# Output tiles in token halves of 64: one gate operation for each PSUM bank, and each half split when it is complete

## The chip, the cores and the metric

The kernel runs on one core of a Trainium2 chip. The time is the device time of one execution in microseconds, the median of several runs; lower is better. TensorE does the matrix products, VectorE (DVE) and ScalarE (ACT) the elementwise work on SBUF and PSUM, GpSimd (POOL) some elementwise work on SBUF, and SyncE (SP) issues almost all DMAs. Each engine takes its instructions in the order in which the program wrote them.

## The reference

Two branches over the same 2048 tokens of 576 channels are mixed by a sigmoid gate. The first is a long convolution (a state-space kernel built from its parameters and applied by a Fourier transform). The second, cut to what matters:

```
s1, s2 = scores of 32 heads against 64 + 64 keys;  top 2 of each, best 2 of the 4 sums
top_e  = expert number (of 4096) of the 2 chosen per head, g = softmax of their scores
act = gelu(einsum("nd,nhkd->nhk", x, u[top_e]))
b   = einsum("nhk,nhk,nhkd->nd", g, act, v[top_e])
out = gate * a + (1 - gate) * b
```

Nothing is gathered. The kernel multiplies every token with all 4096 experts, applies GELU to all of it, multiplies by a gate matrix that is zero except at the chosen experts, and multiplies the result with all rows of `v`.

## The kernel before

The order of all instructions is set by a planner in the program itself. Generators wait for estimated ready times (`ready`), for free buffers (`need`, `take`, `free`) and are resumed by `pump` as the planner's clock advances with each matmul; costs of VectorE, ScalarE, GpSimd and DMA are estimated by the small functions at the top. The resulting order is fixed when the program is built; on the chip only semaphores decide the times.

The work around the change:

- The activations `a` (token tile against experts) are computed as 128 x 512 matmuls, scaled out of PSUM into `go` and stored to a DRAM scratch tensor `g_d` with shape [16 token tiles, 128, 32, 128]: expert row in the partition, 32 expert blocks, 128 tokens.
- `gating` makes, for each token tile, the transposed lists of chosen experts and their weights by small matmuls against an identity; `turned` copies them to `idxT` (partition: head and choice in two token groups; 64 columns).
- `prep(t)` makes the weights of one output tile of 128 tokens. It loads the tile of `g_d` into two slots `gl`, applies GELU on ScalarE, and in four quarters builds one-hot operands (`onehot`: `A`, `Be`, `Bg` on VectorE), multiplies them on TensorE into two PSUM banks `S` of 512 columns (the gates of 16 columns for all 4096 experts), and multiplies the banks into `gl` on VectorE. At the end the product is split into a high and a low float16 part `wh` by `split` (ScalarE the high part, VectorE the remainder; for the first two tiles in some cases ScalarE and GpSimd), and `st[t]` says that the tile is ready.
- The main loop multiplies `wh` of one tile with `v` (`vhl`, 8 chunks, themselves split from the raw rows; the last comes through the slot `vs`) into two banks `o`: 32 blocks x 3 products x 2 halves of the channels = 192 matmuls for a tile. Between blocks it calls `pump`, so that selections `S` of later tiles and the `y` matmuls of the convolution come between the products.
- There are 9 slots ("slot") for `gl`, `wh` and the operands of the earlier stages; one tile needs two for `gl` and two for `wh`.

The tiles are taken in the order 0, 15, 1, 14 and so on. "First", "second", "third" tile below is by this order. All helper calls of VectorE, ScalarE and GpSimd carry line 134 in the profile, all matmuls line 214, all DMAs line 205.

Of the kernel before, what the change touches and what calls it, by code (L numbers as in the profile page):

```python
# [12 lines left out]
F32 = mybir.dt.float32  # L13
# [125 lines left out]
def body(ctx: ExitStack, tc: tile.TileContext, xT, au, par, logdt, dskip, gatew, wq, kT, uT, vv,  # L139
# [60 lines left out]
    def dma(o, i, q=None):  # L200
        t = max(clock[0], rdy.get(key(i), 0.0), queue[0])
        queue[0] = t + 0.45
        wire[0] = max(wire[0], t) + (2 if o.dtype in (F16, BF16) else 4) * o.shape[0] * size(o) / 3.4e5
        rdy[key(o)] = max(rdy.get(key(o), 0.0), wire[0] + 2.2)
        (q or DQ).dma_start(o, i)

    def mm(o, l, r, start, stop, cost=None):
        m = l.shape[0] > 64, 128 if size(l) > 64 else size(l)
        if m != tiling[0]:
            tiling[0] = m  # L210
            clock[0] += 0.13 if m == (True, 128) else 0.1
        clock[0] += (size(r) * (4 if r.dtype == F32 else 1) / 2400 + 0.003) if cost is None else cost
        rdy[key(o)] = clock[0] + 0.4
        T.matmul(o, l, r, start=start, stop=stop)  # L214

    def spawn(gen, after=0.0):
        heapq.heappush(heap, (clock[0] + after, nseq[0], gen))
        nseq[0] += 1
# [16 lines left out]
    def ready(*xs, late=0.0):  # L235
        while True:
            t = max(rdy.get(key(x), 0.0) for x in xs) + late - clock[0]
            if t <= 0:
                return
            yield t  # L240
# [740 lines left out]
    def gating(c):  # L981

        while taken[c] < 4 or not ff:
            yield 0.5
        vv_ = vals[:, :, 8 * c:8 * c + 8].rearrange("p t (h s) k -> p t h s k", s=2)
        ii = idx[:, :, 8 * c:8 * c + 8].rearrange("p t (h s) k -> p t h s k", s=2)
        tl = lambda nm, *z: ff.tile([128, NT, 4, *z], F32, tag="gg" + nm, name=f"gg{nm}{c}")
        a0, a1, b0, b1 = vv_[:, :, :, 0, 0], vv_[:, :, :, 0, 1], vv_[:, :, :, 1, 0], vv_[:, :, :, 1, 1]
        u, w, s, d = tl("u"), tl("w"), tl("s"), tl("d")
        i1, i2, ib = tl("i1", 2), tl("i2", 2), tl("ib", 2)  # L990
        G.tensor_add(u, a0, b1)
        G.tensor_add(w, a1, b0)
# [24 lines left out]
        V.tensor_scalar(ib, ib, MAGIC, MAGIC, op0=OP.add, op1=OP.subtract)  # L1017
        V.scalar_tensor_tensor(i1, i2, 64.0, i1, op0=OP.mult, op1=OP.add)
        fl = lambda x: x.rearrange("p t h k -> p t (h k)")
        V.scalar_tensor_tensor(place[0][:, :, 8 * c:8 * c + 8], fl(ib), -128.0, fl(i1), op0=OP.mult, op1=OP.add)  # L1020
        S.activation(place[1][:, :, 8 * c:8 * c + 8], fl(ib), AF.Copy)
        V.tensor_scalar(u, d, 1.0, None, op0=OP.add)
        V.reciprocal(u, u)
        V.tensor_scalar(u, u, 2.0 ** 14, None, op0=OP.mult)
        pr = prob[:, :, 8 * c:8 * c + 8].rearrange("p t (h k) -> p t h k", k=2)
        yield from ready(u)
        S.activation(pr[:, :, :, 0], u, AF.Copy)
        G.tensor_mul(pr[:, :, :, 1], u, d)
        if c < 7:
            spawn(gating(c + 1))  # L1030
            return
        gated.append(1)
        yield from ready(vals)
        for t in range(NT):
            yield from need("wb")
            p = bank("wb", f"tr{t}")
            for r, x, i in ((0, place[0][:, t], identb), (1, place[1][:, t], identb), (2, prob[:, t], ident)):
                for hh in range(2):
                    mm(p[64 * hh:64 * hh + 64, 64 * r:64 * r + 64], x, i[:, 64 * hh:64 * hh + 64], True, True,
                       0.12 if r == 2 else 0.04)  # L1040
            spawn(turned(t, p))
            del p

# [436 lines left out]
    st = {}  # L1480
# [14 lines left out]
    def prep(t):  # L1495
        while stored[t // 4] < 32:
            yield 1
        yield from need("slot", 2)
        gl = [slot([16, 128], F32, f"gl{t}_{h}") for h in range(2)]
        for h in range(2):  # L1500
            dma(gl[h], g_d[t][:, 16 * h:16 * h + 16])
        while t not in placed:
            yield 0.3
        oh = {0: onehot(t, 0), 1: onehot(t, 1)}
        yield from ready(*gl)
        for h in range(2):
            for b0 in (0, 8):
                g = gl[h][:, b0:b0 + 8]
                S.activation(g, g, AF.Gelu_apprx_tanh)
        for q in range(4):  # L1510
            A, Bg = oh.pop(q)
            yield from ready(A, Bg)
            yield from need("wb", 2)
            pbs = []
            for hb in range(2):
                pS = bank("wb", f"S{t}_{q}_{hb}")
                for j in range(8):
                    a, k = 4 * hb + j // 2, j % 2
                    for z in range(2):
                        mm(pS[:, 64 * j:64 * j + 64], A[:, a, :, k], Bg[:, z, a, :, k], z == 0, z == 1)  # L1520
                pbs.append(pS)
                del pS
            yield from ready(*pbs)
            for hb, pS in enumerate(pbs):
                n0 = 16 * q + 8 * hb
                pv = pS.rearrange("p (k r b) -> p b r k", r=2, b=32)
                for h in range(2):
                    gv = gl[h].rearrange("p b (r n) -> p b r n", r=2)[:, :, :, n0:n0 + 8]
                    V.tensor_tensor(out=gv, in0=pv[:, 16 * h:16 * h + 16], in1=gv, op=OP.mult)
                free("wb", *gl)  # L1530
            del pbs, pS, pv
            if q < 2:
                oh[q + 2] = onehot(t, q + 2)
        if t != ORDER[-1]:
            spawn(prep(ORDER[ORDER.index(t) + 1]))
        h = []
        for z in range(2):
            yield from need("slot")
            h.append(slot([32, 128], F16, f"wh{t}_{z}"))
        fl = lambda x: x.rearrange("p b n -> p (b n)")  # L1540
        for q in range(4):
            bs = slice(8 * q, 8 * q + 8)
            src = gl[q // 2][:, 8 * (q % 2):8 * (q % 2) + 8]
            if t in ORDER[:2] and V.free > clock[0] + 6 and max(G.free, S.free) < clock[0] + 1:
                S.activation(fl(h[0][:, bs]), fl(src), AF.Copy, scale=s_wg)
                S.activation(fl(src), fl(src), AF.Copy, scale=s_wg)
                yield from ready(h[0], *gl)
                G.tensor_sub(fl(h[1][:, bs]), fl(src), fl(h[0][:, bs]))
            else:
                yield from split(fl(h[0][:, bs]), fl(h[1][:, bs]), fl(src), s_wg)  # L1550
            yield 0.3
        free("slot", h[1])
        free("slot", h[1])
        st[t] = h

    yt = {}

    def y_part():
# [281 lines left out]
```

## Time and profile before

| | |
|---|---|
| median of 3 runs | 1456.58 us (1456.38 to 1456.81) |
| profiled execution | 1458.63 us |
| its span, first to last instruction | 1456.8 us |
| mean granted TensorE clock | 0.998 |
| TensorE busy | 1430.8 us (98%) |
| VectorE busy | 1221.0 us (84%) |
| ScalarE busy | 776.0 us (53%) |
| GpSimd busy | 521.4 us (36%) |

In the profile's rows a group is named by its output and its inputs: `gl<-S,gl` is the gate operation, `S<-Bg,A` a selection matmul, `o<-vhl,wh` a product, `wh<-gl,s_wg,wh` the remainder of a split, `gl<-g_d` the load. A row of the timeline gives the start, the duration of the merged run, the engine, the number of instructions after x, and in brackets the idle time before it with what ended it. A row of a stage gives its length, then for each engine the busy time and the number of instructions, then the granted clock, the share of time that the DMA engines were busy, and GB/s.

### The profile page before, as it was taken

How to read it: one execution, taken by the hardware profiler on the slowest of the kernel's cores; microseconds unless marked ns; L12 is line 12 of the kernel's file. 1: busy time of each engine (PE TensorE's matmuls, PEld its weight loads, DVE VectorE, ACT ScalarE, POOL GpSimd, SP SyncE). 2: the span in 40 equal slices, each digit the busy share in tenths (PEclk: the TensorE clock that was granted, in tenths of full speed). 3: DMA queues.
4: the chain of work that ended last, by engine and by line, in shares of the span. 5: the costliest groups of instructions: out<-in, count | busy, mean ns of one | idle time of the engine just before them, and what ended most of it. 6: DMA issues, size and time to landing. Idle time of an engine off the chain costs nothing.

```text
span 1456.8 us, 36814 instructions
## 1 busy us (share of the span) xinstructions
PE 1430.8 (98%) x14103; PEld 853.9 (59%) x14105; DVE 1221.0 (84%) x4569; ACT 776.0 (53%) x1304; POOL 521.4 (36%) x510
## 2 busy tenths in 40 slices
PE   7999999999999999999999999999899999999998
PEld 3445445555454445455555444447687887888787
DVE  6898889889877996885989898689998988998860
ACT  6346776796685776834556564576333224323310
POOL 0335357536446446210237999623000100110100
PEclk9999999999999999999999999999999999999999
DMA  8235223442434432269486776787343432342400
GB/s 306 77 112 172 88 80 109 126 138 72 129 106 124 116 104 92 62 211 292 157 304 216 266 250 214 255 265 228 130 122 110 140 120 98 125 148 67 157 9 17
DMA packets 134352, 215.44 MB, mean 148 GB/s; under 512 B 10912, under 2 KB 79904, under 8 KB 127776
## 3 DMA queue, kind: packets, MB, share of 16 engines
q1 hardware_dynamic: 134080, 213.01, 45.3%
q8 instruction: 111, 1.82, 0.5%
q14 instruction: 65, 0.53, 0.1%
q10 hardware_dynamic: 96, 0.07, 0.0%
HBM read 141.74 MB, written 71.30 MB: 146 GB/s over the span
## 4 chain that ended last, share of the span: by engine, by line
PE 85%; DVE 5%; DMA 2%; ACT 1%; issue 0%; POOL 0%; SPq 0%; DVEq 0%; POOLq 0%
PE o L214 25%; PE s L214 22%; PE a L214 22%; PE S L214 4%; PE kb L214 2%; PE wb L214 2%; PE pr L214 2%; DMA vn<-in_au_dram 1%; PE y L214 1%; PE kP L214 1%; PE k L214 1%; DVE i L134 1%; PE pv L214 1%; PE u L214 1%; DVE vhl L134 1%; DVE m L134 1%
## 5 line engine op out<-in xcount | busy, mean ns | idle before, releaser
L214 PE MATMUL o<-vhl,wh 128*128 128x288 f16 x3072 | 389.2, 287 | 0.0
L214 PE MATMUL s<-whl,xb 128*128 128x512 f16 x1536 | 365.0, 379 | 0.0
L214 PE MATMUL a<-xb,uhl 128*128 128x512 f16 x1536 | 359.5, 379 | 0.2 <-DVE go L134 0.2
L214 PEld LDWEIGHTS <-wh 128*128 128x128 f16 x3072 | 296.8, 98 | 77.5 <-issue 3.7
L214 PEld LDWEIGHTS <-xb 128*128 128x128 f16 x1792 | 170.6, 98 | 208.5 <-issue 14.3
L214 PEld LDWEIGHTS <-uhl 128*128 128x128 f16 x1536 | 147.1, 98 | 176.3 <-issue 3.2
L134 DVE FIND_INDEX8 i<-m,s 128x8 uint32<-128x64 f32 x1024 | 206.9, 226 | 0.0
L134 ACT ACTIVATE wh<-gl,s_wg 128x1024 f16<-128x1024 f32 x64 | 69.0, 1137 | 203.6 <-DVE gl L134 203.6
L134 DVE MAX8 m<-s 128x8 f32<-128x64 f32 x1024 | 146.4, 217 | 27.1 <-PE s L214 26.6
L134 POOL TENSOR_TENSOR CS<-CS,ex 128x512 f32<-128x512 f32 x72 | 97.9, 1389 | 147.6 <-DVE ex L134 146.2
L134 POOL TENSOR_TENSOR ya<-ya,db 128x576 f32<-128x576 f32 x16 | 31.8, 1995 | 320.3 <-DVE Bg L134 159.2
L134 ACT ACTIVATE go<-a,i_a 128x512 f32<-128x512 f32 x92 | 61.5, 682 | 89.1 <-PE a L214 63.9
L134 DVE TENSOR_TENSOR gl<-S,gl 128x256 f32<-128x256 f32 x256 | 90.3, 416 | 13.5 <-PE S L214 10.1
L134 POOL TENSOR_TENSOR e<-aN,rt 128x512 f32<-128x512 f32 x72 | 83.1, 1174 | 49.9 <-PE kb L214 43.8
L134 DVE SCALAR_TENSOR_TENSOR wh<-gl,s_wg,wh 128x1024 f16<-128x1024 f32 x64 | 91.1, 1455 | 11.3 <-ACT wh L134 11.3
L134 DVE TENSOR_TENSOR Bg<-Be,vals 128x1024 f16<-128x1024 f16 x128 | 91.7, 758 | 2.2
L134 ACT ACTIVATE gl<-gl 128x1024 f32<-128x1024 f32 x64 | 63.4, 1044 | 34.1 <-DMA gl<-g_d 34.1
L214 PE MATMUL S<-Bg,A 128*128 128x64 f16 x2048 | 73.6, 194 | 6.4 <-DVE Bg L134 6.4
L214 PEld LDWEIGHTS <-A 128*128 128x128 f16 x2048 | 71.4, 98 | 11.4 <-DVE Bg L134 4.9
L134 DVE TENSOR_TENSOR A<-iota_a,vals 128x2048 f16<-128x2048 f16 x64 | 77.9, 1218 | 0.0
L134 DVE MATCH_VALUE_LOAD i<-m,s 128x8 f32 x1024 | 76.3, 75 | 0.1
L214 PE MATMUL s<-wrem,xb 128*128 128x512 f16 x256 | 76.2, 379 | 0.0
(206 smaller groups left out, 2156.6 us busy)
## 6 DMA issues: line engine op xcount, KB each, us to landing
g_d<-go SPq DMA_DIRECT2D x128, 256.0 KB, 2.4
gl<-g_d SPq DMA_DIRECT2D x32, 1024.0 KB, 5.5
wq<-in_wq_dram SPq DMA_DIRECT2D x16, 1152.0 KB, 5.6
su_d<-us SPq DMA_DIRECT2D x32, 288.0 KB, 2.6
sk_d<-k1o SPq DMA_DIRECT2D x32, 288.0 KB, 3.7
vn<-in_vv_dram SPq DMA_DIRECT2D x32, 288.0 KB, 4.1
ui<-su_d SPq DMA_DIRECT2D x16, 576.0 KB, 4.0
ki<-sk_d SPq DMA_DIRECT2D x16, 576.0 KB, 5.5
```

Of the source, the lines that this page charges most:

```text
L134: return f(*a, **k)
L214: T.matmul(o, l, r, start=start, stop=stop)
```

## The change

The two tiles `gl` of an output tile now hold 32 expert blocks x 64 tokens each instead of 16 blocks x 128 tokens. The transposed lists are permuted to match (the identity is read in two runs of 32 columns), so that quarters 0 and 1 belong to tokens 0 to 63 and quarters 2 and 3 to tokens 64 to 127. A gate operation then covers a whole bank (512 columns) in one instruction, where two were needed. The load of each half takes 64 of the 128 tokens of every block, so 256 bytes in a row. GELU waits for each half by itself. The split moves into a generator of its own, `weights`, which is started for the first half after quarter 1 and for the second after quarter 3; the two `wh` slots are taken after quarter 1.

```diff
-                    mm(p[64 * hh:64 * hh + 64, 64 * r:64 * r + 64], x, i[:, 64 * hh:64 * hh + 64], True, True,
-                       0.12 if r == 2 else 0.04)
+                    mm(p[64 * hh:64 * hh + 64, 64 * r:64 * r + 64], x,
+                       i.rearrange("p (h r n) -> p r h n", h=2, r=2)[:, hh], True, True, 0.12 if r == 2 else 0.04)
...
-        gl = [slot([16, 128], F32, f"gl{t}_{h}") for h in range(2)]
+        gl = [slot([32, 64], F32, f"gl{t}_{h}") for h in range(2)]
         for h in range(2):
-            dma(gl[h], g_d[t][:, 16 * h:16 * h + 16])
+            dma(gl[h], g_d[t][:, :, 64 * h:64 * h + 64])
...
-        yield from ready(*gl)
         for h in range(2):
-            for b0 in (0, 8):
-                g = gl[h][:, b0:b0 + 8]
+            yield from ready(gl[h])
+            for b0 in (0, 16):
+                g = gl[h][:, b0:b0 + 16]
                 S.activation(g, g, AF.Gelu_apprx_tanh)
+        wh = []
         for q in range(4):
...
+            h = q // 2
             for hb, pS in enumerate(pbs):
-                n0 = 16 * q + 8 * hb
-                pv = pS.rearrange("p (k r b) -> p b r k", r=2, b=32)
-                for h in range(2):
-                    gv = gl[h].rearrange("p b (r n) -> p b r n", r=2)[:, :, :, n0:n0 + 8]
-                    V.tensor_tensor(out=gv, in0=pv[:, 16 * h:16 * h + 16], in1=gv, op=OP.mult)
-                free("wb", *gl)
+                n0 = 16 * (q % 2) + 8 * hb
+                gv = gl[h].rearrange("p b (r n) -> p b r n", r=2)[:, :, :, n0:n0 + 8]
+                V.tensor_tensor(out=gv, in0=pS.rearrange("p (k r b) -> p b r k", r=2, b=32), in1=gv, op=OP.mult)
+                free("wb", gl[h])
             if q < 2:
                 oh[q + 2] = onehot(t, q + 2)
+            if q == 1:
+                for z in range(2):
+                    yield from need("slot")
+                    wh.append(slot([32, 128], F16, f"wh{t}_{z}"))
+                spawn(weights(t, 0, wh, gl[0]))
         if t != ORDER[-1]:
             spawn(prep(ORDER[ORDER.index(t) + 1]))
...
+        spawn(weights(t, 1, wh, gl[1]))
+
+    def weights(t, h, wh, g):
+        yield from ready(g)
+        for b in (slice(0, 16), slice(16, 32)):
+            hi, lo = (x[:, b, 64 * h:64 * h + 64] for x in wh)
+            src = g[:, b]
             if t in ORDER[:2] and V.free > clock[0] + 6 and max(G.free, S.free) < clock[0] + 1:
...
+                yield from split(hi, lo, src, s_wg)
             yield 0.3
-        free("slot", h[1])
-        free("slot", h[1])
-        st[t] = h
+        free("slot", wh[1])
+        if h:
+            while t not in half:
+                yield 0.3
+            st[t] = wh
+        half.append(t)
```

Because the planner decides by estimated times, the change also moves other instructions. Three places follow; the number in a name counts the buffer.

TensorE, right after the last `a` matmul of the kernel. Before, quarter 2 of the second tile comes next, ahead of the first product:

```order
L214 LDWEIGHTS wrem_115
L214 MATMUL a_2_3_13269<-xb_519,wrem_115 128x512
L214 LDWEIGHTS A_2_13201
L214 MATMUL S_2_0_13290<-Bg_2_13205,A_2_13201 128x64
L214 LDWEIGHTS A_2_13201
L214 MATMUL S_2_0_13290<-Bg_2_13205,A_2_13201 128x64
```

In the order of the changed kernel the products of the first tile come next:

```order
L214 LDWEIGHTS wrem_115
L214 MATMUL a_2_3_13287<-xb_519,wrem_115 128x512
L214 LDWEIGHTS wh_0_12862
L214 MATMUL o_0_13386<-vhl_9611,wh_0_12862 128x288
L214 LDWEIGHTS wh_0_12862
L214 MATMUL o_1_13387<-vhl_9611,wh_0_12862 128x288
```

All four quarters of the second tile have moved in among the `a` matmuls, and the four quarters of the third tile come after 48, 54, 90 and 120 products, where quarter 0 came after 138 before and quarter 2 after 186.

VectorE, after the last gates of the first tile before (`gl` 12637 and 12638 are its two halves, `wh` 13018 and 13019 its weights): the one-hot operands of the second tile come first, then the four remainders.

```order
L134 TENSOR_TENSOR gl_1_12638<-S_3_1_12992,gl_1_12638 128x32x8
L134 TENSOR_TENSOR A_0_13025<-iota_a,vals 128x2048
L134 TENSOR_TENSOR Be_0_13027<-iota_b,vals 128x1024
L134 TENSOR_TENSOR Bg_0_13029<-Be_0_13027,vals 128x1024 x2
L134 TENSOR_TENSOR A_1_13032<-iota_a,vals 128x2048
L134 TENSOR_TENSOR Be_1_13034<-iota_b,vals 128x1024
L134 TENSOR_TENSOR Bg_1_13036<-Be_1_13034,vals 128x1024 x2
L134 SCALAR_TENSOR_TENSOR wh_1_13019<-gl_0_12637,s_wg,wh_0_13018 128x1024 x2
```

In the changed kernel two of the remainders stand among the gates of the second half, and a gate operation covers a whole bank:

```order
L134 TENSOR_TENSOR gl_1_12638<-S_2_0_12892,gl_1_12638 128x64x8
L134 TENSOR_TENSOR gl_1_12638<-S_2_1_12909,gl_1_12638 128x64x8
L134 SCALAR_TENSOR_TENSOR wh_1_12863<-gl_0_12637,s_wg,wh_0_12862 128x16x64
L134 TENSOR_TENSOR gl_1_12638<-S_3_0_12960,gl_1_12638 128x64x8
L134 TENSOR_TENSOR gl_1_12638<-S_3_1_12977,gl_1_12638 128x64x8
L134 SCALAR_TENSOR_TENSOR wh_1_12863<-gl_0_12637,s_wg,wh_0_12862 128x16x64
L134 SCALAR_TENSOR_TENSOR vhl_12510<-vhl_12511,sci,vhl_12510 128x576
L134 TENSOR_TENSOR A_0_13022<-iota_a,vals 128x2048
```

One remainder of each of the first two tiles moves to GpSimd.

SP, around the load of the third tile (`gl` 13436 and 13437 before, 13348 and 13349 after). Before, it comes after the last chunk of `v` (`vs`) and the first loads for `y`:

```order
L205 DMA g_d<-go_2_2_13279 128x4x128
L205 DMA vs<-in_vv_dram 128x4x576
L205 DMA g_d<-go_2_3_13330 128x4x128
L205 DMA db<-in_dskip_dram 128x576
L205 DMA ya_13355<-in_au_dram 32x576 x4
L205 DMA ya_13360<-in_au_dram 32x576 x4
L205 DMA yz_13365<-z_d 128x1x576 x4
L205 DMA tf_13370<-in_tf_dram 128x256
L205 DMA gl_0_13436<-g_d 128x2048
```

In the changed kernel it comes ahead of them, and `vs` moves behind the first loads for `y`:

```order
L205 DMA gl_0_13348<-g_d 128x32x64
L205 DMA gl_1_13349<-g_d 128x32x64
L205 DMA vhl_12954<-in_vv_dram 128x4x576
L205 DMA g_d<-go_2_2_13340 128x4x128
L205 DMA g_d<-go_2_3_13372 128x4x128
L205 DMA db<-in_dskip_dram 128x576
L205 DMA ya_13396<-in_au_dram 32x576 x4
L205 DMA ya_13401<-in_au_dram 32x576 x4
L205 DMA yz_13406<-z_d 128x1x576 x4
L205 DMA tf_13411<-in_tf_dram 128x256
L205 DMA vs<-in_vv_dram 128x4x576
```

More of the change, by code (lines that the diff above doesn't have):

```diff
@@ L1523, in prep @@
             yield from ready(*pbs)
+            h = q // 2
             for hb, pS in enumerate(pbs):
-                n0 = 16 * q + 8 * hb
-                pv = pS.rearrange("p (k r b) -> p b r k", r=2, b=32)
-                for h in range(2):
-                    gv = gl[h].rearrange("p b (r n) -> p b r n", r=2)[:, :, :, n0:n0 + 8]
-                    V.tensor_tensor(out=gv, in0=pv[:, 16 * h:16 * h + 16], in1=gv, op=OP.mult)
-                free("wb", *gl)
-            del pbs, pS, pv
+                n0 = 16 * (q % 2) + 8 * hb
+                gv = gl[h].rearrange("p b (r n) -> p b r n", r=2)[:, :, :, n0:n0 + 8]
+                V.tensor_tensor(out=gv, in0=pS.rearrange("p (k r b) -> p b r k", r=2, b=32), in1=gv, op=OP.mult)
+                free("wb", gl[h])
@@ L1532, in prep @@
+            del pbs, pS
             if q < 2:
                 oh[q + 2] = onehot(t, q + 2)
+            if q == 1:
[3 more added lines that the diff above has]
+                spawn(weights(t, 0, wh, gl[0]))
         if t != ORDER[-1]:
             spawn(prep(ORDER[ORDER.index(t) + 1]))
[L1536 to L1543, printed above, removed]
+        spawn(weights(t, 1, wh, gl[1]))
[4 more added lines that the diff above has]
+            src = g[:, b]
             if t in ORDER[:2] and V.free > clock[0] + 6 and max(G.free, S.free) < clock[0] + 1:
[L1545 to L1548, printed above, removed]
+                S.activation(hi, src, AF.Copy, scale=s_wg)
+                S.activation(src, src, AF.Copy, scale=s_wg)
+                yield from ready(wh[0], g)
+                G.tensor_sub(lo, src, hi)
@@ L1549, in prep @@
             else:
-                yield from split(fl(h[0][:, bs]), fl(h[1][:, bs]), fl(src), s_wg)
+                yield from split(hi, lo, src, s_wg)
             yield 0.3
-        free("slot", h[1])
-        free("slot", h[1])
-        st[t] = h
+        free("slot", wh[1])
[4 more added lines that the diff above has]
+        half.append(t)
+    half = []
     yt = {}
```

## The prediction

> **What bounds the kernel now.** I read the page first, then the busy time by stages, the waits of TensorE, and the two engines row by row where it waits.
>
> ```profile
> span 1456.8 us, 36814 instructions
> PE 1430.8 (98%) x14103; PEld 853.9 (59%) x14105; DVE 1221.0 (84%) x4569; ACT 776.0 (53%) x1304; POOL 521.4 (36%) x510
> 40.00:940.00 900.00, 893.30 (x8248) 445.87 (x8249) 772.53 (x3842) 569.00 (x1054) 465.60 (x474) 1.00 0.48 154
> 940.00:970.00 30.00, 28.98 (x246) 15.16 (x244) 25.07 (x35) 21.66 (x36) 8.79 (x6) 1.00 0.84 273
> 1000.00:1030.00 30.00, 25.06 (x284) 19.52 (x282) 29.90 (x38) 13.61 (x16) 10.43 (x6) 0.96 0.85 277
> 1030.00:1060.00 30.00, 30.00 (x344) 23.08 (x342) 28.25 (x48) 9.61 (x10) 0.00 (x0) 0.93 0.15 48
> 1180.00:1210.00 30.00, 30.00 (x358) 24.18 (x359) 27.02 (x42) 8.17 (x8) 2.82 (x2) 1.00 0.50 159
> PE S L214 <- DVE Bg L134: 6.4, 4, 4.6
> L214 PE MATMUL o<-vhl,wh 128*128 128x288 f16 x3072 | 389.2, 287 | 0.0
> ```
>
> TensorE is busy for 98% of the span. In the output stage, once it runs evenly (1180 to 1210), it is busy for 30 us of 30, while VectorE has 3 us to spare. So cheaper gates on VectorE bring nothing there. What can move is the transition (950 to 1040): there VectorE is full (29.90 of 30) and TensorE waits 6.4 us in all, four times, always for one-hot operands `Bg` that VectorE has not made yet.
>
> ```profile
> 963.98 1.10 PE L214 MATMUL S<-Bg,A 128*128 128x64 f16 x31 [1.02 <-DVE Bg L134]
> 1011.83 2.15 PE L214 MATMUL y<-yz,tf 128*32 128x288 f32 x32
> 1019.53 3.84 PE L214 MATMUL o<-vhl,wh 128*128 128x288 f16 x30
> 1027.94 0.23 PE L214 MATMUL S<-Bg,A 128*128 128x64 f16 x1 [4.57 <-DVE Bg L134]
> 1028.53 1.81 PE L214 MATMUL S<-Bg,A 128*128 128x64 f16 x31 [0.36 <-DVE Bg L134]
> 1030.16 5.95 PE L214 MATMUL o<-vhl,wh 128*128 128x288 f16 x30
> 1035.94 1.13 PE L214 MATMUL S<-Bg,A 128*128 128x64 f16 x32
> ```
>
> These are quarter 2 of the first tile (1.02 us late) and quarter 2 of the third tile (4.57 and 0.36): 5.95 us. After the long wait 30 products took 5.95 us instead of 3.84, and 31 selections 1.81 instead of 1.13: another 2.8 us at a lower granted clock (0.96 and 0.93 in the two stages). After the 1.02 us wait they took 1.10, full speed. [...]
>
> **The change part by part.** The products, selections and `y` products keep their number and size. What moves is their order in TensorE's queue, and what VectorE has ahead of them. From the first gate to the operands of the third tile's quarter 2, VectorE has 98 instructions in the order before and 69 in the order after. TensorE, from its first selection up to that same quarter, has 320 selections and 151 `a` matmuls in both, but 186 products and 16 `y` matmuls before (the order's count) and 90 products and none after.
>
> *TensorE comes earlier.* One product costs 389.2 / 3072 = 0.127 us, so 96 fewer are 12.2 us; the `y` group is 2.15. Before, TensorE came to this quarter at 1019.53 + 3.84 = 1023.4; without its earlier wait of 1.02 that is 1022.4. After it comes at 1022.4 - 12.2 - 2.15 = 1008.0, if nothing stalls it.
>
> *VectorE comes earlier too, by less.* Its groups between 955.8 and 1028.45, and its rows:
>
> ```profile
> L134 DVE SCALAR_TENSOR_TENSOR wh<-gl,s_wg,wh 128x1024 f16<-128x1024 f32 x8 | 13.2, 1674 | 0.0
> L134 DVE SCALAR_TENSOR_TENSOR vhl<-vhl,sci,vhl 128x576 f16<-128x576 f32 x7 | 5.7, 809 | 0.0
> L134 DVE SCALAR_TENSOR_TENSOR vhl<-vs,sci,vhl 128x576 f16<-128x576 f32 x3 | 4.7, 1577 | 0.0
> L134 DVE SCALAR_TENSOR_TENSOR ya<-y,iuk,ya 128x288 f32<-128x288 f32 x4 | 1.9, 504 | 0.0
> L134 DVE TENSOR_SCALAR go<-a,i_a 128x512 f32<-128x512 f32 x1 | 0.7, 742 | 0.0
> L134 POOL TENSOR_TENSOR vhl<-vhl,vhl 128x576 f16<-128x576 f32 x7 | 10.3, 1479 | 33.5 <-ACT vhl L134 29.9 <-issue 3.1 <-POOL vhl L134 0.5
> 955.88 0.42 DVE L134 TENSOR_TENSOR gl<-S,gl 128x256 f32<-128x256 f32 x1 [2.27 <-ACT gl L134]
> 957.49 1.09 DVE L134 TENSOR_TENSOR gl<-S,gl 128x256 f32<-128x256 f32 x3 [1.18 <-ACT gl L134]
> 978.72 2.47 DVE L134 SCALAR_TENSOR_TENSOR wh<-gl,s_wg,wh 128x1024 f16<-128x1024 f32 x2
> 981.84 4.52 DVE L134 SCALAR_TENSOR_TENSOR wh<-gl,s_wg,wh 128x1024 f16<-128x1024 f32 x2
> 992.78 1.41 DVE L134 TENSOR_TENSOR gl<-S,gl 128x256 f32<-128x256 f32 x4
> 1027.19 1.29 DVE L134 TENSOR_TENSOR Bg<-Be,vals 128x1024 f16<-128x1024 f16 x2
> ```
>
> The operands were complete at 1027.19 + 1.29 = 1028.5. Gone from in front of them are two `wh` splits (2 x 13.2/8 = 3.3), the three `vs` splits (4.7), one `vhl` split (0.8), four `ya` sums (1.9) and one `go` copy (0.7): 11.4 us.
>
> The gates of nine quarters: four operations took 1.41. Two of 512 elements are not in the trace; the nearest is the `go` copy, also 512 from PSUM, 0.742, twice 1.48 and less where they overlap: no gain. If only the elements counted beyond a fixed part they would be about 1.2: a gain of 1.9 in nine. I take 0.6, near the row, and keep 0 to 1.9.
>
> GpSimd now makes two of the `wh` remainders. By its row each is 1479 x 1024/576 = 2.6 us. While GpSimd works VectorE slows: two `wh` splits took 4.52 at 981.84 and 2.47 at 978.72. So this costs VectorE between 0 and 5.2; half, 2.6, is my value.
>
> *The loads of `gl` start the chain later.*
>
> ```profile
> g_d<-go SPq DMA_DIRECT2D x128, 256.0 KB, 2.4
> gl<-g_d SPq DMA_DIRECT2D x32, 1024.0 KB, 5.5
> 939.16 0.85 SPq L205 DMA_DIRECT2D gl<-g_d  x1
> 947.47 0.33 SPq L205 DMA_DIRECT2D gl<-g_d  x1
> 953.55 3.90 ACT L134 ACTIVATE gl<-gl 128x1024 f32<-128x1024 f32 x4
> 1190.00 15.74 SPq L205 DMA_DIRECT2D gl<-g_d  x2
> 1217.83 1.41 DVE L134 TENSOR_TENSOR gl<-S,gl 128x256 f32<-128x256 f32 x4
> ```
>
> A half is now 32 runs of 256 B in each partition, 4096 runs, where it was 128 runs of 8 KB. Also each half needs all 32 blocks of its tile stored, so the first half waits as the second did: it issues at 947.47, not 939.16. How long 4096 short runs take no row shows. Below: 5.5 us, the same bytes. Above: a `g_d` store moves 512 runs of 512 B in 2.4; eight times that is 19.2, too much since each 2.4 has its own start and end. I take 10, since the queues are 0.84 busy in this stage. The first half lands at 957.5, its two GELUs (3.90/4 each) end at 959.5, and VectorE starts 2.4 us late against 957.1 (its 957.49 less the 0.42 done ahead).
>
> [...]
>
> Sum: VectorE is ready 11.4 + 0.6 - 2.6 - 2.4 = 7.0 us earlier, at 1021.5. TensorE comes at 1008.0 and waits 13.5 us on the way there (in pieces, from the second tile on, since nothing else is between), where it waited 5.95: 7.5 us more. One slow-clock stretch stays, 2.8 as before.
>
> *What costs nothing.* ScalarE's splits and GELUs stay 64 of each but for two extra scalings, each like a GELU; it idles most of the even stage (8.17 of 30). There the `gl` loads issue 12 to 28 us ahead of their gates (1190.00 and 1205.7 against 1217.83), and the second half is now wanted two quarters later: 19.2 is covered for the first half, and nearly so for the second. If that cover went, each late us would stop a quarter on TensorE. In SP's queue the third tile's loads move ahead of the last `vhl` chunk and of `vs`, which wait behind them for a free slot; `vs` feeds the last four blocks of the first tile, and TensorE is by then 13 us late itself. The strided identity in `gating` touches 96 small matmuls: nothing. The end after the last product is unchanged.
>
> **The rivals.** *Faster.* The third tile's quarter moved behind VectorE's worst stretch in one point: four `ya` products on GpSimd no longer need to fall before it. With the load at 5.5 us (no delay, and the 1.18 us wait gone), no cost from GpSimd and gates at 1.2, VectorE gains 11.4 + 1.9 + 1.2 = 14.5 and is ready at 1014.0: a wait of 6.0, as before. It turns faster from there on. If GpSimd's absent `ya` work gives back up to 4 us more and the shorter waits leave the clock alone (2.8), it is 7 us faster: 1449.6. For it: the `wh` row of 4.52. Against: two splits were put on GpSimd instead. Chance 0.22.
>
> *No change.* Both shifts cancel, VectorE ready within 3 us of 1014: 1454 to 1459. Chance 0.17.
>
> *The loads bind.* If 19.2 us held and loads went one after another, 38.4 us of loading stands against a tile of 192 x 0.127 + 4 x 1.13 = 28.9: 9.5 us for each of some 14 tiles, 1590. Against: the queues are only half busy (0.50) there. Chance 0.06, with everything above 1474.
>
> **How the numbers follow.** The profiled execution took 1458.63 us, its span 1456.8; the median of the runs is 1456.58, so I add to the median: 1456.6 + 7.5 = 1464. The forecast's own range is 1459.5 to 1474, chance 0.55: from a third of the added wait, up to a landing of 15 us (5 more), all of GpSimd's 5.2 (2.6 more) and a second slow-clock stretch (2.8). The range for 8 in 10 reaches down into the faster case, 1453, and leaves out 0.13 below and 0.06 above. A measurement here can tell about 0.2%, 2.9 us. Faster 0.22, same 0.17, slower 0.55 + 0.06 = 0.61.
>
> **What would show it.** Right: TensorE's waits for `Bg` in the output stage grow from 6.4 to about 13 us, the first of them ahead of the first product, VectorE full to about 1020, and no waits after 1100; `gl` landing near 10. The first step is wrong if `gl` lands in 6 us; the second if VectorE has the third tile's quarter 2 before 1014; the whole if waits for `gl` or `wh` show in each later tile.

## The result and the profile after

The change made the kernel slower: 1471.0 us (median of five runs, 1469.2 to 1472.4) against 1456.4, a ratio of 1.0101 with a 95% interval of 1.0086 to 1.0116, or 14.6 us. The forecast was 7.5 us slower; the direction held and the time lies in the range, but the forecast was half of what came.

The profiled run of the changed kernel took 1469.2 us, the shortest of the five. From the stages of its span, the columns as before (TensorE, its weight loads, VectorE, ScalarE, GpSimd; granted clock; DMA share; GB/s):

```profile
1000.00:1030.00 30.00, 23.30 (x256) 17.76 (x254) 29.82 (x34) 19.37 (x24) 13.14 (x8) 0.89 0.95 235
1030.00:1060.00 30.00, 26.75 (x273) 18.70 (x271) 24.48 (x30) 13.07 (x16) 7.68 (x5) 0.89 0.87 196
sum 1468.00, PE 1435.67 PEld 855.37 DVE 1212.45 ACT 782.36 POOL 527.46; mean PE 205.10 PEld 122.20 DVE 173.21 ACT 111.77 POOL 75.35
```

The granted clock is 0.89 in both stages from 1000 to 1060, where it was 0.96 and 0.93. TensorE is busy for 1435.67 us of the span, 4.9 more than before for the same instructions. The waits of TensorE in the output stage (total, number, longest):

```profile
PE S L214 <- DVE Bg L134: 8.1, 10, 2.4
PE o L214 <- POOL vhl L134: 3.2, 2, 2.2
PE S L214 <- DVE gl L134: 0.5, 1, 0.5
```

11.8 us of waits stand where 6.4 stood. Span, busy time and these waits close: before 1456.8 - 1430.8 - 6.4 = 19.6, after 1467.1 - 1435.7 - 11.8 = 19.6. So the profiled difference of 10.3 us is 5.4 us of waits and 4.9 us of longer busy time. About 3 of the 4.9 are slow clock, by the rows below and those of before: the slow rows take 5.9 us more than the same work at full speed, where before they took 2.8. About 1 more is an estimate for selections that start anew behind a wait: the first of them stands alone with 0.20 us, while 32 in a row take 1.13. The rest is not accounted for. (The other 4 us of the 14.6 lie between runs: the profiled run of before, 1458.6, was longer than its timed runs, that of after the shortest of its five. What they hold no trace shows.) Where they lie, in TensorE's rows (start, us, operation, and in brackets the idle time ahead of it):

```profile
1005.41 0.20 PE L214 MATMUL S<-Bg,A 128*128 128x64 f16 x1 [1.07 <-DVE Bg L134]
1007.98 1.81 PE L214 MATMUL S<-Bg,A 128*128 128x64 f16 x31 [2.36 <-DVE Bg L134]
1009.60 1.63 PE L214 MATMUL o<-vhl,wh 128*128 128x288 f16 x6
...
1019.82 0.20 PE L214 MATMUL S<-Bg,A 128*128 128x64 f16 x1 [2.18 <-DVE Bg L134]
1020.42 1.09 PE L214 MATMUL S<-Bg,A 128*128 128x64 f16 x31 [0.40 <-DVE Bg L134]
1021.35 5.51 PE L214 MATMUL o<-vhl,wh 128*128 128x288 f16 x30
...
1038.32 2.73 PE L214 MATMUL o<-vhl,wh 128*128 128x288 f16 x12 [2.19 <-POOL vhl L134]
1042.11 11.11 PE L214 MATMUL o<-vhl,wh 128*128 128x288 f16 x76 [1.06 <-POOL vhl L134]
```

One selection quarter after another waits 0.2 to 2.4 us, and behind some of the waits the work runs slowly: 31 selections in 1.81 us instead of 1.10, 6 products in 1.63 (0.90 at full speed, by rows of the same trace), 30 in 5.51 (3.84), 12 in 2.73 (1.64), and the last row too, with 76 products in 11.11 where 96 take 11.92 later. At 1038 and 1042 the products wait for `vhl`, the last block group made from `vs`. Nothing waits after 1060.

The granted clock shows where it was slow. The stages are cut here so that each is wholly slow or wholly fast:

```profile
1004.54:1007.95 3.41, 0.20 (x1) 0.12 (x2) 3.38 (x4) 3.41 (x5) 2.70 (x2) 1.00 1.34 218
1007.95:1011.36 3.41, 3.25 (x37) 2.36 (x36) 3.38 (x3) 2.72 (x4) 1.11 (x1) 0.50 1.33 220
1014.77:1018.19 3.42, 2.87 (x24) 2.06 (x21) 3.38 (x6) 2.89 (x6) 1.74 (x2) 1.00 0.44 132
1018.19:1021.61 3.42, 1.39 (x35) 1.25 (x36) 3.42 (x5) 0.76 (x3) 1.03 (x1) 1.00 0.70 224
1021.61:1025.02 3.41, 3.41 (x17) 2.16 (x15) 3.38 (x5) 2.84 (x3) 0.49 (x1) 0.50 0.85 242
1035.26:1038.67 3.41, 1.22 (x11) 0.85 (x9) 2.82 (x2) 3.41 (x5) 1.65 (x1) 1.00 0.78 223
1038.67:1045.50 6.83, 5.77 (x26) 3.46 (x24) 6.83 (x7) 2.18 (x4) 5.17 (x3) 0.50 1.02 224
```

The same of the kernel before:

```profile
1027.64:1034.47 6.83, 6.17 (x51) 4.39 (x52) 6.79 (x15) 0.00 (x0) 0.00 (x0) 0.50 0.30 128
```

There are three slow stretches, of 3.41, 3.41 and 6.83 us, all at half clock; before there was one of 6.83. In the 3.41 us ahead of each TensorE had been busy for only 0.20, 1.39 and 1.22 us. Behind a stretch with 2.87 us of work the clock stayed full.

The rows of the other engines, from the same timeline: VectorE's first two gates of 512, its operands of the third tile's quarter 2, SP's issue of the third tile's loads and of `vs`, and ScalarE's first work on `vs`; the last row is SP's issue of `vs` in the kernel before:

```profile
957.18 1.29 DVE L134 TENSOR_TENSOR gl<-S,gl 128x512 f32<-128x512 f32 x2 [6.03 <-ACT gl L134]
1018.12 2.25 DVE L134 TENSOR_TENSOR Bg<-Be,vals 128x1024 f16<-128x1024 f16 x2
999.79 4.87 SPq L205 DMA_DIRECT2D gl<-g_d  x2
1024.32 0.43 SPq L205 DMA_DIRECT2D vs<-in_vv_dram  x1
1033.33 1.44 ACT L134 ACTIVATE vhl<-vs,sci 128x576 f16<-128x576 f32 x2 [8.88 <-DMA vs<-in_vv_dram]
```

```profile
992.71 0.51 SPq L205 DMA_DIRECT2D vs<-in_vv_dram  x1
```

And the gate loads in the view of the DMA issues (KB each, median us to landing):

```profile
gl<-g_d SPq DMA_DIRECT2D x32, 1024.0 KB, 9.4
```

### The profile page after: what moved, and what is told of

Its sections match the earlier page's. It is cut to its first block, busy times and chain, and to the rows that moved or that the text cites. A ratio compares the mean times of both kernels' runs of the same rounds, so it can differ in the third digit from the quotient of the medians.

```text
span 1467.1 us, 36658 instructions
## 1 busy us (share of the span) xinstructions
PE 1435.7 (98%) x14103; PEld 855.4 (58%) x14105; DVE 1212.5 (83%) x4436; ACT 782.4 (53%) x1309; POOL 527.5 (36%) x514
## 4 chain that ended last, share of the span: by engine, by line
PE 83%; DVE 5%; DMA 4%; ACT 1%; SPq 1%; issue 1%; POOL 0%; DVEq 0%; ACTq 0%; POOLq 0%
PE o L214 24%; PE s L214 22%; PE a L214 21%; PE S L214 4%; PE kb L214 2%; PE wb L214 2%; PE pr L214 2%; DMA g_d<-go 1%; DVE i L134 1%; PE kP L214 1%; PE k L214 1%; PE y L214 1%; PE pv L214 1%; PE u L214 1%; DMA vhl<-in_vv_dram 1%; DVE m L134 1%
## 5 line engine op out<-in xcount | busy, mean ns | idle before, releaser
L134 DVE TENSOR_TENSOR gl<-S,gl 128x512 f32<-128x512 f32 x128 | 82.0, 682 | 35.9 <-ACT gl L134 28.2
L134 DVE TENSOR_TENSOR Bg<-Be,vals 128x1024 f16<-128x1024 f16 x128 | 96.1, 792 | 2.2
L134 DVE TENSOR_TENSOR A<-iota_a,vals 128x2048 f16<-128x2048 f16 x64 | 82.9, 1296 | 0.0
L134 DVE SCALAR_TENSOR_TENSOR wh<-gl,s_wg,wh 128x1024 f16<-128x1024 f32 x62 | 78.7, 1296 | 4.5 <-ACT wh L134 4.5
L214 PE MATMUL a<-xb,wrem 128*128 128x512 f16 x256 | 75.9, 379 | 0.0
```

The lines of the kernel that those rows point to most:

```text
L134: return f(*a, **k)
```

## The experiments

After these traces I had three theories. **O**, the order: the early split pulls the third tile's quarters ahead of VectorE, and pushes `vs` behind its loads. **L**, the loads: 4096 runs of 256 bytes land late. **G**, GpSimd's remainders slow VectorE's selection operands. After the first four runs O and L were joined to **OL**: each costs about half. Where an expectation gives the products ahead of the third tile's quarter 2 as 168 in the order before or with the late split, or as 222 in the held kernel of before, the rows have 186 and 240: it leaves out the 18 that stand ahead of the second tile's last quarter.

The ratios of the experiments are to the kernel before, run beside them on the same chip (its medians were 1456.7 to 1457.0 us there). For each kernel I add its profiled run's waits of TensorE in the output stage and its busy time over the span. A profiled run of an experiment is one of its timed runs, and not always near their median: that of run 6 took 3.1 us more, that of run 8 was the shortest of twelve, 3.2 us less.

| run | us | ratio, 95% interval | waits | busy |
|---|---|---|---|---|
| before | 1456.4 | 1 | 6.4 | 1430.8 |
| the change | 1471.0 | 1.0101 (1.0086 to 1.0116) | 11.8 | 1435.7 |
| late split | 1465.4 | 1.0051 (1.0030 to 1.0071) | 12.1 | 1430.6 |
| before, short loads | 1462.3 | 1.0035 (1.0023 to 1.0047) | 7.4 | 1431.7 |
| the change, long loads | 1462.6 | 1.0039 (1.0024 to 1.0055) | 8.0 | 1430.5 |
| third tile held | 1468.1 | 1.0074 (1.0050 to 1.0098) | 14.1 | 1432.8 |
| `vs` first, held | 1474.4 | 1.0113 (1.0093 to 1.0133) | 16.0 | 1434.6 |
| half-major, late split | 1461.5 | 1.0028 (1.0015 to 1.0041) | 8.8 | 1432.3 |
| before, held | 1453.2 | 0.9979 (0.9964 to 0.9995) | 0.7 | 1427.6 |
| half-major, late split, held | 1458.3 | 1.0015 (1.0002 to 1.0029) | 5.6 | 1429.8 |
| no remainders on GpSimd | 1470.1 | 1.0088 (1.0064 to 1.0111) | 13.7 | 1432.7 |
| loads priced | 1466.2 | 1.0066 (1.0046 to 1.0087) | 11.2 | 1430.8 |
| before, short loads, held | 1465.2 | 1.0055 (1.0036 to 1.0074) | 10.2 | 1432.6 |
| late split, held | 1459.7 | 1.0016 (1.0004 to 1.0028) | 5.8 | 1430.5 |

**1. Late split.** Both halves are split after the last quarter, as before; the rest of the change stays.

```
-            if q == 1:
-                ... two wh slots ...; spawn(weights(t, 0, wh, gl[0]))
...
+        ... two wh slots ...
+        spawn(weights(t, 0, wh, gl[0]))
         spawn(weights(t, 1, wh, gl[1]))
```

> The changed kernel, but both halves of a tile's split start only when all four quarters of the tile are gated, as in the kernel before; token-half tiles, 512-value gate operations and 256-byte loads stay. The matrix engine's order falls back almost to that of before: vs is issued ahead of the third tile's gate loads, and 168 products instead of 90 stand ahead of the third tile's quarter 2. Theory O (the early split pulls the third tile's quarters ahead of VectorE and pushes vs behind its loads): the waits for vhl (3.2 us) are gone, those for Bg fall from 8.1 to about 6, the granted clock at 1030 to 1060 is back at 0.93 or more; 1456 to 1460 us. Theory L (the loads of 256-byte runs cost the time): 1467 to 1472, since every load stays. Theory G (GpSimd's remainders slow VectorE): between them, about 1463, since one or two remainders stay on GpSimd.

TensorE's waits, and SP's issue of `vs`:

```profile
PE S L214 <- DVE Bg L134: 5.6, 7, 2.8
PE a L214 <- DVE go L134: 4.1, 1, 4.1
```

```profile
996.67 0.92 SPq L205 DMA_DIRECT2D vs<-in_vv_dram  x1
```

1465.4 us, 5.6 less than the change. The waits for `vhl` are gone (`vs` leaves SP at 996.7 instead of 1024.3), those for `Bg` are 5.6, the clock is 1.00 again after 1000 (from 970 to 1000 it is 0.94, behind the wait for `go`) and the busy time is that of before: this much of O holds. The loads, with the same short runs, land in 7.4 us (median) instead of 9.4, so the early split also made the loads slower. But 8.4 us are left to before, with new waits (`go`, 4.1), so O alone is not the cause. The time came out in no theory's band but near G's.

**2. Before, with short loads.** Each gate load of the kernel before is cut into two of 64 tokens; every order stays.

```
-            dma(gl[h], g_d[t][:, 16 * h:16 * h + 16])
+            for z in range(2):
+                dma(gl[h][:, :, 64 * z:64 * z + 64], g_d[t][:, 16 * h:16 * h + 16, 64 * z:64 * z + 64])
```

> The kernel before, with each gate load cut into two of 64 of the 128 tokens, so that the runs in memory are 256 bytes as in the changed kernel; order on every engine as before, two more DMA instructions a tile. Theory L: the loads land near 9 to 10 us after their issue in place of 5.5, and the time goes to 1464 to 1471. Theory O: the first tile's gates start about 4 us later, which is bounded by what VectorE can lose there; 1456 to 1461 us, the rest of the 14.6 us is not seen. Theory G: no change, 1456.

The loads in the view of the DMA issues, then ScalarE's and VectorE's rows for the third tile:

```profile
gl<-g_d SPq DMA_DIRECT2D x64, 512.0 KB, 6.6
```

```profile
1026.63 2.01 ACT L134 ACTIVATE gl<-gl 128x1024 f32<-128x1024 f32 x2 [3.50 <-DMA gl<-g_d]
1032.16 1.29 DVE L134 TENSOR_TENSOR Bg<-Be,vals 128x1024 f16<-128x1024 f16 x2
```

1462.3 us, 5.3 more, between L and O. A load of half the size took 6.6 us to land. VectorE has the operands of the third tile's quarter 2 at 1032.16 + 1.29 = 1033.4, where it had them at 1028.5: 5.0 us later, of which 1.9 stood there already when the first load was issued (941.07 instead of 939.16); ahead of them ScalarE's GELU waited 3.5 us for the load. TensorE came 5.0 us later to that quarter too, and waited there 4.53, as before (4.57).

**3. The change, with long loads.** Every load is one run of 8 KB a partition, at the price that the gates lie at wrong places. (Its first half again needs only half of the stored blocks, so it issues earlier too.)

```
-            dma(gl[h], g_d[t][:, :, 64 * h:64 * h + 64])
+            dma(gl[h] as [p, 2048], g_d[t] as [p, 4096][:, 2048 * h:2048 * h + 2048])
```

> The changed kernel with its gate loads in contiguous runs of 8 KB, as in the kernel before; the values come to lie in the wrong places of the token-half tiles, and everything else, the order included, is that of the changed kernel. Theory L: landing 5 to 6 us again and 1457 to 1461 us. Theory O: landing 5 to 6 us, waits for Bg still 6 to 8 and for vhl still 2 to 3; 1467 to 1471 us. Theory G: 1471.

TensorE's waits, the two stages, and the rows of VectorE and SP:

```profile
PE S L214 <- DVE Bg L134: 5.7, 7, 2.3
PE o L214 <- POOL vhl L134: 2.3, 2, 2.2
```

```profile
1000.00:1030.00 30.00, 24.48 (x291) 18.02 (x290) 29.83 (x37) 16.89 (x21) 12.91 (x7) 0.94 0.66 201
1030.00:1060.00 30.00, 27.66 (x312) 21.53 (x310) 27.96 (x35) 12.32 (x15) 8.16 (x4) 1.00 0.48 160
```

```profile
1015.06 1.29 DVE L134 TENSOR_TENSOR Bg<-Be,vals 128x1024 f16<-128x1024 f16 x2
1016.41 0.43 SPq L205 DMA_DIRECT2D vs<-in_vv_dram  x1
```

1462.6 us, 8.4 less than the change: nearer to L, though loads landed in 7.1 us (median), not in 5 to 6. VectorE has the operands at 1016.35 instead of 1020.37, `vs` issues at 1016.4 instead of 1024.3, and the clock stays at 0.94 and 1.00: 3.8 us of waits and 5.2 of busy time are gone (the two profiled spans differ by 7.7). What remains to before, 5.6 us, is with long loads and the change's order.

**4. The third tile held.** Quarters 2 and 3 of the third tile wait until some expert blocks of the first tile are multiplied.

```
             yield from ready(A, Bg)
+            while t == ORDER[2] and blocks[0] < 24 + 5 * (q - 2):
+                yield 0.3
```

> The changed kernel, with the third tile's quarters 2 and 3 held back until 24 and 29 of the first tile's 32 expert blocks have been multiplied, so that 144 products instead of 90 stand ahead of quarter 2 (54 more by 0.127 us, 6.9 us of work in place of waiting). The loads, the early split and the late vs stay. Theory O: the waits for Bg fall from 8.1 to 1 to 4 us, those for vhl stay between 0 and 3.2, and with the clock back in one of two slow stretches the time is 1461 to 1467 us. Theory L and theory G: the waits move to other names and the time stays within 3 us of 1471.

TensorE's waits:

```profile
PE o L214 <- DVE vhl L134: 5.7, 2, 5.2
PE S L214 <- DVE Bg L134: 3.1, 5, 1.3
PE o L214 <- POOL vhl L134: 2.3, 1, 2.3
PE o L214 <- ACT vhl L134: 1.0, 1, 1.0
```

1468.1 us, just above O's band and 2.9 from the change, which the two intervals do not tell apart. The waits for `Bg` fell from 8.1 to 3.1 as expected, but those for `vhl` rose to 9.0: `vs` still leaves SP at 1025.3, and products that come sooner reach it sooner. The wait only changed its name.

**5. `vs` first, and held.** So the third tile's loads also wait until `vs` is issued.

```
+        while t == ORDER[2] and 7 not in vs_on:
+            yield 0.3
         yield from need("slot", 2)
         gl = [slot([32, 64], F32, f"gl{t}_{h}") for h in range(2)]
```

> The changed kernel with its early split and its 256-byte loads, but the third tile's gate loads wait until vs has been issued, and the third tile's quarters 2 and 3 until 24 and 29 expert blocks have been multiplied; 168 products stand ahead of quarter 2 instead of 90. Theory OL (order and loads each cost about half): the waits for vhl are gone, those for Bg 2 to 5 us, what is left is what the loads cost in the kernel before, 5.3 us: 1461 to 1465. If loads alone cost: 1469 to 1472. If the order alone costs: 1455 to 1458.

TensorE's waits, SP's issue of the third tile's loads, and the stage after 1030:

```profile
PE S L214 <- DVE Bg L134: 8.7, 9, 2.9
PE y L214 <- DMA tf<-in_tf_dram: 6.0, 1, 6.0
```

```profile
1014.60 10.37 SPq L205 DMA_DIRECT2D gl<-g_d  x2
```

```profile
1030.00:1060.00 30.00, 22.22 (x242) 17.27 (x241) 29.83 (x36) 14.76 (x17) 6.33 (x4) 0.77 0.73 162
```

1474.4 us, a miss by nine, and no gain over the change. `vs` issued at 1014.2, ten sooner, but the third tile's loads went 15 us later (1014.6 in place of 999.8), 7.1 of the 8.7 us of waits for `Bg` stand behind that, and from 1030 on the clock fell to 0.77. Ahead of them TensorE waited 6.0 us for `tf`, whose load SP issues behind the others. In the code `vs` waits for a free slot, and an early split takes its two slots sooner; with the late split `vs` left at 996.7. Putting it first only made the third tile and the `y` group wait.

**6 and 7. Half-major storage with a late split, without and with a hold.** The gates are stored half by half, so that each load is one run of 8 KB and every value is in its place; each store becomes two. The hold is that of run 4, at blocks 40 and 45.

```
-    g_d = dr.tile([NT, 128, 32, 128], F32, name="g_d")
+    g_d = dr.tile([NT, 128, 2, 32, 64], F32, name="g_d")
...
-        dma(g_d[4 * tb:4 * tb + 4, :, 4 * c + j, :]..., go)
+        for h in range(2):
+            dma(g_d[4 * tb:4 * tb + 4, :, h, 4 * c + j, :]..., go[:, :, 64 * h:64 * h + 64])
...
-            dma(gl[h], g_d[t][:, :, 64 * h:64 * h + 64])
+            dma(gl[h], g_d[t][:, h])
```

> The changed kernel with the gates stored in memory half by half (each store of an activation bank becomes two, in runs of 256 bytes instead of 512; each gate load is one run of 8 KB), and with the split started only after the last quarter, as before. Of the change there remain the token-half tiles, the 512-value gate operations and the loads that need the last store. Theory OL: both costs are gone, loads land in 5 to 7 us, 1455 to 1459 us. If a third cost remains (GpSimd's remainders, the 512-value operations): 1461 or more.

> The gates stored half by half and the late split, as in the run beside it, and the third tile's quarters 2 and 3 held until 40 and 45 blocks. Theory OL: 1447 to 1453 us, beside the held kernel of before, the waits in the output stage below 3 us. Rival, the wait only moves: as the same kernel without the hold, 1455 to 1459.

Of the kernel without the hold, TensorE's waits and the gate loads in the view of the DMA issues:

```profile
PE S L214 <- DVE Bg L134: 5.9, 7, 1.8
PE y L214 <- DMA tf<-in_tf_dram: 2.9, 1, 2.9
```

```profile
gl<-g_d SPq DMA_DIRECT2D x32, 1024.0 KB, 5.7
```

1461.5 and 1458.3 us, both above OL's bands and in those of the rivals: a third cost remains (1461 or more), and the wait only moves (1455 to 1459). The loads land in 5.7 us again. `Bg` still holds TensorE for 5.9 us, and the `y` group waits 2.9 for `tf` (3.4 in the held kernel), which SP issues at 1014.8. With both suspected costs taken out 4.8 us still stand (2.2 to 6.0 by the interval of the ratio). The doubled stores (256 of 128 KB), the loads that need the last store, the 512-value operations, GpSimd's remainders or the later start of the output stage's loads may make it; the runs do not separate them, and this share stays open.

**8. Before, held.** The kernel before, with the hold at blocks 40 and 45.

> The kernel before, with only the third tile's quarters 2 and 3 held until 40 and 45 blocks (the first product loop has 32, so all of the first tile's products stand ahead of quarter 2, 222 instead of 168). Theory OL: before's own wait of 4.6 and the slow stretch after it go, 1448 to 1453 us. Rival: the wait only moves to a later quarter or to the next tile, 1455 to 1458.

TensorE's only wait for `Bg`, and its rows at the third tile's quarter 2:

```profile
PE S L214 <- DVE Bg L134: 0.4, 1, 0.4
```

```profile
1029.12 1.13 PE L214 MATMUL S<-Bg,A 128*128 128x64 f16 x32
1030.09 3.84 PE L214 MATMUL o<-vhl,wh 128*128 128x288 f16 x30
```

1453.2 us, at the upper edge of its band, and the one kernel that beats both: 0.9979 (0.9964 to 0.9995), or 3.5 us (0.7 to 5.2). The third tile's quarter 2 comes at 1029.1 with its operands made, 30 products take 3.84 us, the clock is 1.00. In the profiled runs waits are down by 5.7 and busy time by 3.2, more than the 3.5 us between the medians: the profiled run was the shortest of its twelve, that of before longer than its median. So before's wait and slow stretch did go, and 3.5 us is what the runs show them to be worth.

**9. No remainders on GpSimd.** `if False:` in place of the condition in `weights`.

> The changed kernel with no split remainder on GpSimd (ScalarE's extra scaling goes too; VectorE takes the remainders at 1.28 us each). The third tile's quarter 2 stands 12 products later, vs is still behind the third tile's loads. Theory G (GpSimd's remainders slow VectorE's selection operands by some 2.6 us each): 1466 to 1469 us. Theory OL: within 2 us of 1471, since neither the loads nor the place of vs changes.

TensorE's row at the third tile's quarter 2:

```profile
1020.85 1.59 PE L214 MATMUL S<-Bg,A 128*128 128x64 f16 x31 [1.47 <-DVE Bg L134]
```

1470.1 us, 0.9 from the change, within its uncertainty, and above G's band, though the interval (1466 to 1473) reaches into it: the run gives G no support as the cause, and does not rule out a small share. VectorE makes the remainders itself, and quarter 2 of the third tile gets under way no sooner (1020.85 in this row of TensorE, 1020.42 in the change). The slowing itself is in the change's trace: while GpSimd made a remainder (1005.25 to 1007.38) VectorE took 3.26 us for two `Bg`, where it takes 1.29 at 1010.78. But in this run `Bg` is slow as well (2.38 and 3.33 us), beside GpSimd's `vhl` operations (from 1005.86 and 1015.78 on), so taking the remainders away did not take the slowing away.

**10. Loads priced.** The planner counts 4 us more for a gate load: `rdy[key(gl[h])] += 4.0` behind the `dma` in `prep`.

> The changed kernel, with 4 us added to the landing time that the planner counts for a gate load, which is about what the traces show it to be short of; no instruction is added. The planner then puts 198 products instead of 90 ahead of the third tile's quarter 2, and vs ahead of the third tile's loads. Theory OL: the order's share goes, the waits for Bg fall to 2 to 5 us and those for vhl are gone, 1459 to 1464 us. If the hold's miss above shows that no order helps while vs waits for a slot: 1469 to 1473.

1466.2 us, 4.8 less than the change, but above the band: the waits for `vhl` are all but gone (0.3), those for `Bg` are 8.5, the longest 3.2, at other quarters (970 and 1037). The planner can be told when a load lands; that it still does not know how late VectorE is, is my reading of the waits that remain.

**11 and 12. The hold with short loads, on before and on the late split.** The hold of run 8 on the kernels of runs 2 and 1.

> The held kernel of before (1453.2 us) with its gate loads cut into runs of 256 bytes. If the loads cost by making VectorE 4 to 5 us later at the third tile's quarter 2: a wait of 4 to 5 us comes back there, with the slow stretch behind it 1458 to 1461 us. If they cost only where before's order had a wait anyway: 1452 to 1455.

> The changed kernel with the late split (1465.4 us) and the third tile's quarters 2 and 3 held until 40 and 45 blocks. Theory OL: its waits for Bg of 5.6 us fall below 3, the wait for go of 4.1 stays, 1458 to 1462 us. If the waits only move: 1464 to 1467.

The waits of the first, and a row of TensorE in it:

```profile
PE S L214 <- DVE Bg L134: 10.2, 12, 2.9
```

```profile
1091.50 0.24 PE L214 MATMUL S<-Bg,A 128*128 128x64 f16 x1 [2.86 <-DVE Bg L134]
```

The held kernel of before took 1465.2 us with short loads, 12 more and above both bands; no wait came back at the third tile's quarter 2. The waits stand in later tiles (1091, 1153 and others). After 1060 the longest single wait of ScalarE for a gate load is 3.7 us in the kernel before, 5.6 with short loads, 10.6 with the hold and 12.3 with both (in sum 34.1, 46.4, 34.3 and 53.3). I read this so that the hold had used up the lead of the loads, and short ones then come too late for VectorE and TensorE; no run tests that by itself. What the runs show is that the loads' price depends on the order around them: 5.3 us in before's, 8.4 in the change's, 12 in the held one. The late split with the hold took 1459.7 us, in its band, but not by the waits expected: those for `Bg` fell from 5.6 only to 4.1 (below 3 was expected), that for `go` from 4.1 to 1.7, and in all from 12.1 to 5.8.

**What follows.** Two causes are shown. Taking the short loads out of the change brings 8.4 us (run 3), taking the early split out 5.6 (run 1), of 14.6 (by the ratios, 9.0 and 7.3). Run 3 also lets the first half's load go out earlier, so its gain is not that of the run length alone. They are not a clean sum: each acts through the same waits between 980 and 1045 and the slow clock behind them, each makes the loads land later (medians: 9.4 us in the change, 7.1 and 7.4 with one of them out, 5.7 with both), and with both out 4.8 us remain (run 6). In all runs span less busy time less waits is 19.5 to 21.7 us, so at most some 2 us hide anywhere else: what the change costs is wait or longer busy time.

## Why the prediction was right, and where not

*The bound, and where to look*: right. Everything lies between 980 and 1045, and nothing waits after 1060; the even stage covered the longer loads.

*VectorE comes earlier, by 7.0 us*: right in sum, 8.1 (1020.4 instead of 1028.5, forecast 1021.5), but not in its terms, so the sum was partly luck. The late loads were put at 2.4 us for the first tile, where they cost nothing: VectorE's first gates start at 957.18, against 957.1 before. They cost it later, where the sum had no term: ScalarE waits for the loads of the second and third tile too, and VectorE then waits 3.0 us for ScalarE between 970 and 1000. In all they cost VectorE 4.0 us by run 3 against the change and 5.0 by run 2, or 4.9 and 3.1 when both runs are set to the issue of the last store ahead of the first load. GpSimd's two remainders, put at 2.6 us, slowed VectorE by some 3.9 by the rows beside them (2.62 us in place of 0.68 for `Be` at 976.61, 3.26 in place of 1.29 for `Bg` at 1004.66); run 9 shows no gain in time without them. The gates lay in the range that was kept: two of 512 took 1.29 us in place of four in 1.41, 1.1 us in nine quarters where 0.6 was taken.

*Loads land near 10 us*: right for the median, 9.4, but not for the load that the sum was about: the first half of the first tile landed 7.5 us after its issue. Loads issued alone landed in 6.8 to 7.4 (at 1069.7, 1094.9, 1107.3 and 1117.5). Of the two loads at 1148, issued 0.6 us apart as the change often does, the first landed in 9.3, the second in 13.4.

*TensorE's wait of 13.5 in place of 5.95*: the wait came in pieces, as said, but they add to 8.6 us up to the third tile's quarter 2, and those for `Bg` to 8.1 in all, where about 13 was named as the sign of being right. With the 3.2 for `vhl` the waits grew by 5.4 us, not 7.5, and the longer busy time stands beside them.

*One slow stretch stays, 2.8*: wrong, and the term that was mis-sized most: no further loss was in the sum (the range allowed for one more stretch), and busy time grew by 4.9 us, some 3 of it slow clock. The 2.8 us are those of the kernel before; that just one stretch stays when the wait comes in pieces was the author's estimate, and no run shows it. In the changed kernel no piece is longer than 2.4 us, and three stretches ran at half clock behind them, 13.65 us in place of 6.83. In the 3.41 us ahead of each, the pieces had left 0.20, 1.39 and 1.22 us of work. The length of a piece alone did not sort them: behind one of 2.18 us 30 products took 5.51 us here, behind one of 2.76 in run 1 they took 3.84.

*`vs` costs nothing, since TensorE is 13 us late itself*: wrong. `vs` issued at 1024.3 (before 992.7), ScalarE had it at 1033.3, and products waited 3.2 us for it and ran slowly behind. `vs` came 32 us later, more than the 13 us that were to cover it.

So the direction was forecast for the right reason, work pulled ahead of VectorE, and the time lies in the range; but 7.5 us were half of it, since the two terms put at nothing (`vs`, and further slow clock) were not nothing.

The rival "faster" had part of its mechanism right (VectorE did come earlier), but VectorE was ready at 1020.4 and not at 1014.0, and the shorter waits did not leave the clock alone. "The loads bind" did not come about at 9.4 us; in run 11, with the hold, waits do appear in later tiles.

## What to carry to other kernels

Where a planner orders the work, a change of a transfer's shape is a change of the order's assumptions: price the shape in the planner, and look at what moved in the queues (here `vs`, 32 us) before costing the operations. Pulling work ahead on the bound engine did not pay here, where the engine that feeds it was not as far ahead (TensorE's waits went from 6.4 to 11.8 us); a hold at one place of the kernel before (0.9979) was worth more than cheaper gates. And waits can cost more than their length (here they grew by 5.4 us, and the busy time of the same instructions by 4.9, some 3 of it slow clock), so sum the busy time of equal work beside the waits.

## What was not expected of the hardware

- Waits of 0.2 to 2.4 us, with single selections between them, went with a granted clock of 0.89 over 60 us. (The 0.77 over 30 us in run 5 stands behind waits of up to 2.9 us.) In the changed kernel the slow stretches there are at 0.50, last 3.41, 3.41 and 6.83 us and start at 1007.95, 1021.61 and 1038.67, so 13.66 and 17.06 us apart, 4 and 5 times 3.41 within 0.02; the one of the kernel before starts at 1027.64 and lasts 6.83.
- Both traces can be cut into steps of 3.41 us from these starts (from 30 us after the start on, leaving out the last steps). In the changed kernel TensorE was busy for 0.20, 1.39 and 1.22 us in the three steps at full clock that a slow one followed, and for at least 2.09 (at 857.77) in all others; in the kernel before for 0.00 in the one, and for at least 1.76 (at 454.20) in all others. The length of a wait alone does not sort the cases. In the changed kernel waits of 2.18 and 0.40 us left 1.39 us of work in one step, and 30 products took 5.51 us instead of 3.84 behind them. In run 10, behind waits of 2.48 and 0.39 us, 30 products took 3.84. In run 2 a wait of 4.53 cost less than in the kernel before: 30 products in 4.43 behind it, not 5.95.
- 1024 KB in 4096 runs of 256 bytes landed in 6.8 to 7.4 us when issued alone and in up to 13.7 as the second of two; the median was 9.4 in the change and 7.4 with the late split. In 128 runs of 8 KB the median was 5.5 to 5.8, and 7.1 in run 3. Between 1000 and 1030 the share of busy DMA engines rose from 0.85 to 0.95 while the rate fell from 277 to 235 GB/s; other transfers of that stage had moved as well, so this is not the run length alone.
